# Gated attention and a feed-forward layer: K' turned by VectorE and DRAM instead of TensorE

## The chip, the cores and the metric

The kernel runs on one core of a Trainium2 chip. The metric is the device time of one launch in microseconds: 521.53 us in the median of three runs. The core has five engines that work side by side, each with a queue of its own in a fixed order: TensorE (PE, matrix products; its weight loads are shown as PEld), VectorE (DVE), ScalarE (ACT), GpSimd (POOL) and SyncE (SP), which here only issues transfers. Engines wait for each other by semaphores.

## The reference

```python
def _attn_ref(q, k, v, alpha):          # B, H, S, D = 4, 8, 768, 48
    for t in range(S):
        state = alpha[:, :, t, :, None] * state + np.einsum('bhd,bhe->bhde', k[:, :, t], v[:, :, t])
        y[:, :, t] = np.einsum('bhd,bhde->bhe', q[:, :, t], state)

def _moe_ref(x, w_in, w_out):           # 3072 x 384, 384 x 2048, 2048 x 384
    h = x @ w_in
    g = np.where(h >= 1, h, np.where(h <= -1, 0.0, (h + 1) ** 2 / 4))
    return g @ w_out
```

The output of the attention, laid as 3072 tokens of 384 numbers, is the x of the feed-forward layer. All inputs are fp32.

## The kernel before, in words

The 3072 tokens are 24 chunks of 128, counted from 0 here. For each chunk `prepare` loads alpha, k and q (`raw` tiles, eight buffers). From chunk 7 on (`EARLY`) they lie in DRAM with d at partitions; the chunks before are laid with the tokens at partitions, and `turned` transposes them on TensorE into PSUM (`flip`, L486). Two scans on VectorE make the running products of alpha, forward into `Q` (L547) and backward into `inv` (L573); `inv` times k is K' (L587) and `Q` times q is Q' (L593, POOL, or DVE in chunks 1 to 6).

The state update needs K' with tokens at partitions. `begin_chunk` transposes it on TensorE (`turn_keys`, L614, four matrix products against an identity), and ACT copies it from PSUM to the tile `ks` (L617). Then comes a burst of small products on TensorE: `update` (L642, `ks` with v), `scores` (L629) and, from chunk 7 on, the `outputs` (L769) of the chunk before. DVE adds the updates to `state` (L671) and masks the scores (L715); ACT and DVE split the outputs into two parts of fp32r in `ring` (L793, L798), and when a group of three chunks is complete six transfers within `ring` (L814) put the rest of it in its place.

The feed-forward layer works on groups of three chunks and sixteen blocks f of 128 hidden units. One step f is a hidden product on TensorE (`hidden`, L865: nine matrix products of 384 columns from `ring` into a `ps_h` bank), the activation (DVE clips, L909; ACT squares, L894; DVE takes the max, L920, into `gf`; ACT casts, L924, and POOL subtracts, L925, into `gh`), and a second product (`second`, L943: nine matrix products of `gh` with w_out). The second product of a step is given a due time `LAG` = 3 steps behind its hidden product, and `gf` and `gh` have three buffers. Groups 0 and 1 take eight blocks in turn, since the weights are still being fetched and decoded on ACT, DVE and POOL (L365 to L420); the others take sixteen.

What stands when on an engine is decided at build time: `Plan` collects all steps with a cost in us, a due time (in steps f) and what they read and write, and `order` runs a list scheduling over the five engines, with buffers, PSUM banks and the port that DVE and POOL share. Some steps may go to one of two engines (`other`). While TensorE would stand idle in the first part, fillers without use (L1014, `fill`) are put in its queue. SP issues all transfers in one queue.

Of the kernel before, what the change touches and what calls it, by code (L numbers as in the profile page):

```python
# [8 lines left out]
F32 = mybir.dt.float32  # L9
# [17 lines left out]
GROUP = 3  # L27
SHARE = 2
EARLY = 7
MORE = 2  # L30
WARM = 15
LAG = 3.0
FETCH = 12.0
LOAD = 4.0
DECODE = 3.0
PREPARE = 2.5
# [196 lines left out]
def gated_attention_ffn(ctx: ExitStack, tc: tile.TileContext, q, k, v, alpha, laid, out):  # L233
# [77 lines left out]
    with ExitStack() as main:  # L311
# [4 lines left out]
        def pool(name, **kw):  # L316
            pools[name] = main.enter_context(tc.tile_pool(name=name, bufs=1, **kw))
# [146 lines left out]
        def load(x, j, key):  # L464

            raw = raws[x, j] = buf("stage", "raw", [P, G * CH], 8)
            plan.op(
                "SP",
                Plan.ISSUE,
                key,  # L470
                lambda: nc.sync.dma_start(out=raw(), in_=laid[("tok_" if j < EARLY else "dim_") + x][j]),
                [],
                [raw],
                moved=P * G * CH * 4,
            )

        def turned(x, j, key, to=()):

            raw = raws[x, j]
            if j < EARLY:  # L480
                ps = ps_a(j)
                view = lambda: flat(ps())

                def flip():
                    for g in range(G):
                        nc.tensor.transpose(  # L486
                            out=view()[:, g * CH : (g + 1) * CH],
                            in_=raw()[:, g * P : (g + 1) * P],
                            identity=ident,
                        )  # L490
# [7 lines left out]
        def prepare(j, key):  # L498
# [85 lines left out]

            vec(0.15, lambda: nc.vector.reciprocal(out=meet[:, j, 1], in_=inv()[:, :, 0]), [inv], [("meet", j, 1)], False)
            kt, kT = turned("k", j, key + 0.2)
            vec(0.66, lambda: nc.vector.tensor_tensor(out=flat(inv()), in0=flat(inv()), in1=kT(), op=ALU.mult), [inv, kt], [inv])  # L587
# [5 lines left out]
            mul = lambda e: e.tensor_tensor(out=flat(Q()), in0=flat(Q()), in1=qT(), op=ALU.mult)  # L593
            in_ps = QHELP <= j < EARLY
            ways = [("DVE", 0.66, lambda: mul(nc.vector), not in_ps), ("POOL", 1.3, lambda: mul(nc.gpsimd), True)]
            (e, us, emit, port), other = ways if in_ps else reversed(ways)
# [4 lines left out]
        others, meets, turnt = {}, {}, {}  # L601
        group_of = [max(n for n in range(NG) if first[n] <= j) for j in range(NCH)]

        def begin_chunk(j, key):

            Q, K, _ = prepared[j]

            other = others[j] = buf("att", "other", [P, G, CH], 2)
            kp, ks = ps_a(j), buf("att", "ks", [P, G, P], 1)
            turnt[j] = ks  # L610

            def turn_keys():
                for g in range(G):
                    nc.tensor.transpose(out=kp()[:, g], in_=K()[:, g], identity=ident)  # L614

            plan.op("PE", 0.45, key - 0.1, turn_keys, [K], [kp, ks], mode="full")
            plan.op("ACT", 0.6, key, lambda: nc.scalar.copy(out=ks(), in_=kp()), [kp], [ks])  # L617

            meets[j] = [ps_a(j, 512) for _ in range(2)]
# [17 lines left out]
        def update(j):  # L637
            for g in range(G):
                for u in range(1 + ((j + 1) % PER != 0)):
                    for r in range(2):  # L640

                        nc.tensor.matmul(  # L642
                            out=up(j, u)[64 * r : 64 * r + 64, g],
                            lhsT=turnt[j]()[halves[u], g, 64 * r : 64 * r + 64],
                            rhs=V[j]()[halves[u], 2 * g + r],
                            start=True,
                            stop=True,
                        )
# [174 lines left out]
        def attend(j, key):  # L823

            begin_chunk(j, key)
            Q, K, _ = prepared[j]
            ks, vt = turnt[j], V[j]
            if j > MERGE:
                ps = ps_a(j)

# [21 lines left out]
        def hidden(n, f, key, c0=0, c1=GROUP):  # L852
# [1 line left out]
            c1 = min(c1, groups[n])  # L854
            L = (c1 - c0) * CH
            h = bank("ps_h", 2, [P, L])
            gf, gh = buf("fw", "gf", [P, L], 3), buf("fw", "gh", [P, 2, L], 3, F32R)
            xs = [("x", j % (2 * GROUP)) for j in range(first[n] + c0, first[n] + c1)]
            at = slice(span(n).start + c0, span(n).start + c1)

# [160 lines left out]
        for j in range(NCH):  # L1021
            n = max(n for n in range(NG) if first[n] <= j)
            since = begin[n - 1] if n > 0 else begin[n] - AHEAD
            due = since + (begin[n] - since) * (j - first[n] + 1) / groups[n] - (MARGIN, MARGIN0, MARGIN1)[n + 1 if n < 2 else 0]
            prepare(j, due - PREPARE)
            attend(j, due)
            done = j if j < MERGE or j == NCH - 1 else j - 1
            while at < len(segs) and first[segs[at][0]] + groups[segs[at][0]] - 1 <= done:
# [214 lines left out]
```

## Time and profile before

| | us |
|---|---|
| three runs: median (lowest to highest) | 521.53 (520.77 to 521.73) |
| span of the profiled execution, first to last instruction | 520.1 |
| PE busy in that span | 498.7 (96%) |
| DVE busy | 359.6 (69%) |
| ACT busy | 262.8 (51%) |
| POOL busy | 262.9 (51%) |

The profiled execution has no time of its own beside its span; the span is 1.4 us below the median of the runs. Busy times of PE are intervals that overlap, as its matrix products are pipelined, so what a piece of its work costs is read from starts: from one instruction's start to the next one's. In rows of a timeline the columns are start, length, engine, line, operation, output and inputs, count, and in brackets how long the engine stood idle before it and who ended that. In rows of groups they are count, busy us, mean ns, then idle time ahead. The granted clock of TensorE is 0.998 in the mean.

### The profile page before, as it was taken

The numbers are of one execution on the slowest core, as the hardware profiler recorded it, in microseconds if no ns is written. First come the engines' busy times: TensorE is split into PE (matmuls) and PEld (weight loads), VectorE is DVE, ScalarE is ACT, GpSimd is POOL, SyncE is SP. The second block draws the span as 40 slices with busy tenths as digits, with TensorE's granted clock in tenths as the row PEclk, the third lists the DMA queues.
The fourth block names the chain that finished last, engine by engine and source line by source line (L and its number), as shares of the span: only waits on it lengthen the run. The fifth ranks groups of instructions, "written<-read, shape, count | busy, mean of one in ns | idle before, by whom it ended". The sixth has DMA issues, their size and how long they took to land.

```text
span 520.1 us, 12248 instructions
## 1 busy us (share of the span) xinstructions
PE 498.7 (96%) x4861; PEld 480.4 (92%) x4861; DVE 359.6 (69%) x673; ACT 262.8 (51%) x509; POOL 262.9 (51%) x286
## 2 busy tenths in 40 slices
PE   8889898979999999999999999999999999999995
PEld 7788788978899999999999999999999999999994
DVE  6999999788978757578567757578567775343333
ACT  3899896575543444344444444444444444333331
POOL 3688885899974354254354344254354242323330
PEclk9999999999999999999999999999999999999999
DMA  8997849011435323133123323133102200010001
GB/s 255 378 348 250 316 98 346 3 48 55 122 106 137 109 65 90 48 96 122 43 60 91 112 62 79 56 84 125 56 21 59 67 2 11 15 37 10 0 1 50
DMA packets 27902, 52.46 MB, mean 101 GB/s; under 512 B 3808, under 2 KB 13504, under 8 KB 27840
## 3 DMA queue, kind: packets, MB, share of 16 engines
q1 hardware_dynamic: 27840, 51.62, 31.8%
q8 instruction: 40, 0.66, 0.6%
q14 instruction: 22, 0.18, 0.1%
HBM read 43.65 MB, written 5.90 MB: 95 GB/s over the span
## 4 chain that ended last, share of the span: by engine, by line
PE 79%; DVE 9%; POOL 4%; issue 3%; ACT 3%; DVEq 0%; POOLq 0%; ACTq 0%
PE ps L943 35%; PE ps L865 34%; PE ps L769 4%; PE ps L642 2%; DVE inv L573 2%; POOL gh L925 2%; PE ps L629 2%; PE ps L614 2%; DVE Q L547 1%; POOL w L405 1%; ACT gf L894 1%; DVE w L381 1%; DVE Q L715 1%; POOL wt L420 1%; PE ps L1014 1%
## 5 line engine op out<-in xcount | busy, mean ns | idle before, releaser
L943 PE MATMUL ps<-wt,gh 128*128 128x384 f32 x1152 | 225.3, 340 | 4.3 <-POOL gh L925 3.5
L925 POOL TENSOR_TENSOR gh<-gf,gh 128x384 fp32r<-128x384 f32 (+1 forms) x129 | 146.6, 1141 | 163.6 <-ACT gh L924 117.2
L865 PE MATMUL ps<-ring,wt 128*128 128x384 f32 (+1 forms) x1170 | 223.0, 337 | 2.8 <-DVE inv L573 1.2
L865 PEld LDWEIGHTS ps<-ring,wt 128*128 128x128 f32 x1170 | 203.9, 188 | 4.3 <-issue 1.5
L943 PEld LDWEIGHTS ps<-wt,gh 128*128 128x128 f32 x1152 | 200.5, 188 | 7.2 <-POOL gh L925 5.2
L894 ACT ACTIVATE gf<-gf,half_b 128x384 f32<-128x384 f32 x122 | 74.6, 616 | 120.7 <-DVE gf L909 117.4
L909 DVE TENSOR_SCALAR gf<-ps 128x384 f32<-128x384 f32 x122 | 66.9, 553 | 71.3 <-PE ps L865 62.7
L920 DVE TENSOR_TENSOR gf<-gf,ps 128x384 f32<-128x384 f32 (+1 forms) x130 | 70.3, 543 | 45.1 <-ACT gf L894 44.7
L924 ACT CAST gh<-gf 128x384 fp32r<-128x384 f32 (+1 forms) x130 | 65.7, 507 | 67.8 <-DVE gf L920 61.1
L573 DVE TENSOR_TENSOR_SCAN inv<-raw,bwd 128x511 f32<-128x511 f32 x17 | 34.9, 2052 | 0.0
L405 POOL TENSOR_TENSOR w<-w,wt 128x384 int32<-128x384 int32 (+1 forms) x25 | 31.2, 1261 | 7.0 <-DVE w L392 6.0
L547 DVE TENSOR_TENSOR_SCAN Q<-raw,fwd 128x512 f32<-128x512 f32 x17 | 27.4, 1613 | 7.3 <-PE ps L769 7.2
L420 POOL TENSOR_TENSOR wt<-w,wt 128x384 fp32r<-128x384 f32 (+1 forms) x24 | 31.3, 1318 | 1.7 <-ACT wt L418 1.4
L661 ACT COPY both<-state 48x192 f32<-48x192 f32 x69 | 24.1, 350 | 12.3 <-POOL state L746 9.0
L746 POOL TENSOR_TENSOR state<-state,last 128x192 f32<-128x192 f32 x20 | 11.9, 594 | 34.3 <-DVE state L671 34.1
L769 PE MATMUL ps<-Q,both 128*64 128x64 f32 x372 | 27.1, 225 | 1.4 <-issue 1.4
L769 PEld LDWEIGHTS ps<-Q,both 128*64 128x64 f32 x372 | 23.7, 137 | 4.1 <-issue 2.8
L769 PE MATMUL ps<-other,both 128*64 128x64 f32 x372 | 27.0, 225 | 0.0
L617 ACT COPY ks<-ps 128x512 f32<-128x512 f32 x24 | 14.1, 587 | 21.5 <-PE ps L614 21.4
L715 DVE TENSOR_TENSOR Q<-ps,mask 64x256 f32<-64x256 f32 x48 | 20.3, 423 | 6.5 <-ACT other L679 5.6
L593 POOL TENSOR_TENSOR Q<-Q,raw 128x512 f32<-128x512 f32 x18 | 23.2, 1290 | 2.9 <-DVE inv L565 2.0
L769 PEld LDWEIGHTS ps<-other,both 128*64 128x64 f32 x372 | 23.5, 138 | 0.2 <-ACT both L661 0.2
(79 smaller groups left out, 415.7 us busy)
## 6 DMA issues: line engine op xcount, KB each, us to landing
both<-in_laid_v_both SPq DMA_DIRECT2D x48, 128.0 KB, 3.0
wt<-in_laid_w_in SPq DMA_DIRECT2D x8, 768.0 KB, 7.2
wt<-in_laid_w_out SPq DMA_DIRECT2D x8, 768.0 KB, 7.5
vt<-in_laid_v SPq DMA_DIRECT2D x24, 192.0 KB, 2.9
out<-ot SPq DMA_DIRECT2D x24, 192.0 KB, 2.7
raw<-in_laid_dim_a SPq DMA_DIRECT2D x17, 256.0 KB, 2.9
raw<-in_laid_dim_k SPq DMA_DIRECT2D x17, 256.0 KB, 3.0
raw<-in_laid_dim_q SPq DMA_DIRECT2D x17, 256.0 KB, 2.7
```

The costliest lines, as they stand in the source:

```text
L405: add = lambda e, c=c: e.tensor_tensor(out=bits()[:, c], in0=bits()[:, c], in1=word(I32, 0)[:, c], op=ALU.add)
L420: sub = lambda e, c=c: e.tensor_tensor(out=part(1)[:, c], in0=data()[:, c], in1=part(0).bitcast(F32)[:, c], op=ALU.subtract)
L547: lambda: nc.vector.tensor_tensor_scan(flat(Q()), aT(), flat(fwd), 0.0, ALU.mult, ALU.max),
L573: lambda: nc.vector.tensor_tensor_scan(flat(inv())[:, 0:n][:, ::-1], aT()[:, 1 : n + 1][:, ::-1], flat(bwd)[:, 0:n][:, ::-1], bwd[:, G - 1 ...
L769: nc.tensor.matmul(out=ps()[halves[r], to, halves[u]], lhsT=lhsT[:, r, u], rhs=x()[:, g, halves[u]], start=m + u == 0, stop=True, skip_gro ...
L865: nc.tensor.matmul(out=h(), lhsT=win(f, w)[:, kt], rhs=ring[:, at, kt, a, :], start=(m == 0), stop=(m == 3 * KT - 1),)
L894: lambda: nc.scalar.activation(out=gf(), in_=in_(), func=func, scale=scale, bias=bias),
L909: lambda: nc.vector.tensor_scalar(out=gf(), in0=h(), scalar1=-1.0, scalar2=1.0, op0=ALU.max, op1=ALU.min),
L920: lambda: nc.vector.tensor_tensor(out=gf(), in0=gf(), in1=h(), op=ALU.max),
L924: plan.op("ACT", 0.08 + 0.41 * w, key + 0.4, lambda: nc.scalar.copy(out=gh()[:, 0], in_=gf()), [gf], [gh])
L925: sub = lambda e: e.tensor_tensor(out=gh()[:, 1], in0=gf(), in1=gh()[:, 0].bitcast(F32), op=ALU.subtract)
L943: nc.tensor.matmul(out=o_ps[seg][t](), lhsT=gh()[:, a, (t - c0) * CH : (t - c0 + 1) * CH], rhs=wout(f, w), start=(f == f0 and i == 0), sto ...
```

## The change

K' of chunks 7 to 23 (`TURN` = 7) is no longer turned by TensorE and ACT. `turn_blocks` transposes its sixteen 32x32 blocks on DVE into a tile `part` (L622 of the changed file), writes `part` to a buffer in DRAM (256 KB, L634) and reads it back with four transfers of 32 partitions each, in runs of 512 bytes, into `ks` (L644), which now has two buffers and another order of its columns. All five are issued by SP. The chunks from 7 on are prepared 2.5 steps earlier (`PLACING`). k and q of chunks 2 to 6 are laid with d at partitions, so that only alpha of these chunks is flipped on TensorE; their Q' may now go to DVE or POOL. `LAG` is 4, and `gf` and `gh` have four buffers. The scratch memory that the program reserves for transfers is made smaller.

```diff
+PLACED = {"a": EARLY, "k": 2, "q": 2}
+TURN = 7
+PLACING = 2.5
-LAG = 3.0
+LAG = 4.0
...
+        blocks = [pools["sums"].tile([P, G * CH], F32, name=f"blocks{i}") for i in range(2)]
...
-                lambda: nc.sync.dma_start(out=raw(), in_=laid[("tok_" if j < EARLY else "dim_") + x][j]),
+                lambda: nc.sync.dma_start(out=raw(), in_=laid[("tok_" if j < PLACED[x] else "dim_") + x][j]),
...
-            if j < EARLY:
+            if j < PLACED[x]:
...
-            in_ps = QHELP <= j < EARLY
+            in_ps = QHELP <= j < PLACED["q"]
...
+        def turn_blocks(j, K, ks, key):
+            part = buf("att", "part", [P, 4, 32, G], 1)
+            plan.op(
+                "DVE",
+                0.62,
+                key - PLACING,
+                lambda: nc.vector.transpose(
+                    out=part().rearrange("p j b g -> p j g b"), in_=K().rearrange("p g (j a) -> p j g a", a=32)
+                ),
+                [K],
+                [part],
+                port=True,
+            )
+            placed = lambda: ks().rearrange("p g c -> p (g c)").rearrange("p (c g) -> p c g", g=G)
...
+                lambda: nc.sync.dma_start(out=blocks[j % 2], in_=part().rearrange("p j b g -> p (j b g)")),
...
+            for i in range(4):
...
+                    lambda i=i: nc.sync.dma_start(
+                        out=ks()[32 * i : 32 * i + 32],
+                        in_=blocks[j % 2].rearrange("(i a) (j c) -> j a i c", a=32, c=CH)[i],
+                    ),
...
+            turnt[j] = lambda u, g, r: placed()[halves[u], 64 * r : 64 * r + 64, g], ks
...
-            kp, ks = ps_a(j), buf("att", "ks", [P, G, P], 1)
+            ks = buf("att", "ks", [P, G, P], 2)
+            if j >= TURN:
+                return turn_blocks(j, K, ks, key)
...
-            gf, gh = buf("fw", "gf", [P, L], 3), buf("fw", "gh", [P, 2, L], 3, F32R)
+            gf, gh = buf("fw", "gf", [P, L], 4), buf("fw", "gh", [P, 2, L], 4, F32R)
...
-            prepare(j, due - PREPARE)
+            prepare(j, due - PREPARE - PLACING * (j >= TURN))
...
-    nc = bacc.Bacc("TRN2", target_bir_lowering=False, num_devices=1)
+    nc = bacc.Bacc("TRN2", target_bir_lowering=False, num_devices=1, dynamic_dma_scratch_size=1024)
```

With it the planner's order changes on all engines. First PE around the burst of chunk 14, before (L943 second products, L865 hidden ones, L614 the turn, L642 and L629 the start of the burst):

```order
L943 MATMUL ps<-wt,gh 128x384 x9
L865 MATMUL ps<-ring,wt 128x384 x18
L943 MATMUL ps<-wt,gh 128x384 x18
L865 MATMUL ps<-ring,wt 128x384 x9
L614 MATMUL ps<-ident,inv 128x128 x4
L943 MATMUL ps<-wt,gh 128x384 x9
L865 MATMUL ps<-ring,wt 128x384 x9
L642 MATMUL ps<-vt,ks 64x48 x16
L629 MATMUL ps<-Q,inv 64x64 x16
```

and the same place in the changed kernel (L996 second, L918 hidden, L694 and L681 the start of the burst):

```order
L996 MATMUL ps<-wt,gh 128x384 x9
L918 MATMUL ps<-ring,wt 128x384 x9
L996 MATMUL ps<-wt,gh 128x384 x18
L918 MATMUL ps<-ring,wt 128x384 x18
L996 MATMUL ps<-wt,gh 128x384 x9
L918 MATMUL ps<-ring,wt 128x384 x9
L996 MATMUL ps<-wt,gh 128x384 x9
L694 MATMUL ps<-vt,ks 64x48 x16
L681 MATMUL ps<-Q,inv 64x64 x16
```

The turn is gone, and the burst stands behind the 59th hidden product instead of the 58th.

Then DVE between two bursts, where the first row belongs to the burst's state update and L587 makes K', before (a cycle with the forward scan L547 right behind that update; L715 are the masks):

```order
L671 TENSOR_TENSOR state<-state,ps 128x192
L909 TENSOR_SCALAR gf<-ps 128x384
L551 RECIPROCAL bwd<-Q 128x4
L565 COPY inv<-bwd 128x1
L573 SCALAR_TENSOR_TENSOR inv<-raw,bwd 128x511
L920 TENSOR_TENSOR gf<-gf,ps 128x384
L909 TENSOR_SCALAR gf<-ps 128x384
L585 RECIPROCAL meet<-inv 128x4
L920 TENSOR_TENSOR gf<-gf,ps 128x384
L587 TENSOR_TENSOR inv<-inv,raw 128x512
```

and after, where L962 is the clip, L973 the max, L577 the backward scan, L593 K' and L622 the transposition:

```order
L723 TENSOR_TENSOR state<-state,ps 128x192
L555 RECIPROCAL bwd<-Q 128x4
L569 COPY inv<-bwd 128x1
L962 TENSOR_SCALAR gf<-ps 128x384 x2
L577 SCALAR_TENSOR_TENSOR inv<-raw,bwd 128x511
L589 RECIPROCAL meet<-inv 128x4
L593 TENSOR_TENSOR inv<-inv,raw 128x512
L973 TENSOR_TENSOR gf<-gf,ps 128x384 x2
L622 STREAM_TRANSPOSE part<-inv 128x4x4x32
```

Two clips stand ahead of the backward scan instead of one, none behind it, and the maxes behind K' instead of ahead. In other cycles with ten products one max stands between K' and the transposition.

SP's queue over the same cycle, before:

```order
L519 DMA both<-in_laid_v_both 64x512 x2
L508 DMA vt<-in_laid_v 128x384
L471 DMA raw<-in_laid_dim_q 128x512
L471 DMA raw<-in_laid_dim_a 128x512
L471 DMA raw<-in_laid_dim_k 128x512
L519 DMA both<-in_laid_v_both 64x512 x2
L508 DMA vt<-in_laid_v 128x384
```

and after:

```order
L523 DMA both<-in_laid_v_both 64x512 x2
L512 DMA vt<-in_laid_v 128x384
L475 DMA raw<-in_laid_dim_q 128x512
L475 DMA raw<-in_laid_dim_a 128x512
L475 DMA raw<-in_laid_dim_k 128x512
L634 DMA blocks_108<-part 128x512
L644 DMA ks<-blocks_108 32x4x128 x4
L523 DMA both<-in_laid_v_both 64x512 x2
```

The write and the four reads stand behind the three loads of the next chunk and ahead of the loads of v that wait for the burst.

Last, PE at the start of the group of chunks 9 to 11, behind the burst of chunk 12 (its last product is the first row), before:

```order
L769 MATMUL ps<-other,both 64x64
L865 MATMUL ps<-ring,wt 128x384 x9
L943 MATMUL ps<-wt,gh 128x384 x9
L865 MATMUL ps<-ring,wt 128x384 x9
L943 MATMUL ps<-wt,gh 128x384 x9
L865 MATMUL ps<-ring,wt 128x384 x18
```

and after:

```order
L821 MATMUL ps<-other,both 64x64
L918 MATMUL ps<-ring,wt 128x384 x9
L996 MATMUL ps<-wt,gh 128x384 x27
L918 MATMUL ps<-ring,wt 128x384 x27
L996 MATMUL ps<-wt,gh 128x384 x9
```

The first product of the new group is the second half of the last row before and the first third of the row of 27 after: five products stood between burst and group, now four.

More of the change, by code (lines that the diff above doesn't have):

```diff
@@ L586, in prepare @@
             kt, kT = turned("k", j, key + 0.2)
-            vec(0.66, lambda: nc.vector.tensor_tensor(out=flat(inv()), in0=flat(inv()), in1=kT(), op=ALU.mult), [inv, kt], [inv])
+            vec(
+                0.66,
+                lambda: nc.vector.tensor_tensor(out=flat(inv()), in0=flat(inv()), in1=kT(), op=ALU.mult),
+                [inv, kt],
+                [inv],
+                j >= PLACED["k"],
+            )
             qt, qT = turned("q", j, key + 0.2)
@@ L593, in prepare @@
             mul = lambda e: e.tensor_tensor(out=flat(Q()), in0=flat(Q()), in1=qT(), op=ALU.mult)
-            in_ps = QHELP <= j < EARLY
+            in_ps = QHELP <= j < PLACED["q"]
             ways = [("DVE", 0.66, lambda: mul(nc.vector), not in_ps), ("POOL", 1.3, lambda: mul(nc.gpsimd), True)]
-            (e, us, emit, port), other = ways if in_ps else reversed(ways)
+            (e, us, emit, port), other = ways if QHELP <= j < EARLY else reversed(ways)
             plan.op(e, us, key + 0.3, emit, [Q, qt, last], [Q], port=port, other=None if in_ps else other)
@@ L602, in gated_attention_ffn @@
         group_of = [max(n for n in range(NG) if first[n] <= j) for j in range(NCH)]
+        def turn_blocks(j, K, ks, key):
[10 more added lines that the diff above has]
+                port=True,
+            )
+            placed = lambda: ks().rearrange("p g c -> p (g c)").rearrange("p (c g) -> p c g", g=G)
+            plan.op(
+                "SP",
+                Plan.ISSUE,
+                key - PLACING,
+                lambda: nc.sync.dma_start(out=blocks[j % 2], in_=part().rearrange("p j b g -> p (j b g)")),
+                [part],
+                [("blocks", j % 2)],
+                moved=P * G * CH * 4,
+            )
+            for i in range(4):
+                plan.op(
+                    "SP",
+                    Plan.ISSUE,
+                    key - PLACING,
+                    lambda i=i: nc.sync.dma_start(
+                        out=ks()[32 * i : 32 * i + 32],
+                        in_=blocks[j % 2].rearrange("(i a) (j c) -> j a i c", a=32, c=CH)[i],
+                    ),
+                    [("blocks", j % 2)],
+                    [ks],
+                    moved=P * CH * 4,
+                    beside=i > 0,
+                )
+            turnt[j] = lambda u, g, r: placed()[halves[u], 64 * r : 64 * r + 64, g], ks
         def begin_chunk(j, key):
@@ L608, in begin_chunk @@
             other = others[j] = buf("att", "other", [P, G, CH], 2)
-            kp, ks = ps_a(j), buf("att", "ks", [P, G, P], 1)
-            turnt[j] = ks
+            ks = buf("att", "ks", [P, G, P], 2)
+            if j >= TURN:
+                return turn_blocks(j, K, ks, key)
+            kp = ps_a(j)
+            turnt[j] = lambda u, g, r: ks()[halves[u], g, 64 * r : 64 * r + 64], ks
             def turn_keys():
@@ L617, in begin_chunk @@
             plan.op("ACT", 0.6, key, lambda: nc.scalar.copy(out=ks(), in_=kp()), [kp], [ks])
-            meets[j] = [ps_a(j, 512) for _ in range(2)]
         ss = lambda j, r: meets[j][r]()[:, 0 : G * HC].rearrange("p (g t) -> p g t", g=G)
@@ L643, in update @@
                             out=up(j, u)[64 * r : 64 * r + 64, g],
-                            lhsT=turnt[j]()[halves[u], g, 64 * r : 64 * r + 64],
+                            lhsT=turnt[j][0](u, g, r),
                             rhs=V[j]()[halves[u], 2 * g + r],
@@ L825, in attend @@
             begin_chunk(j, key)
+            meets[j] = [ps_a(j, 512) for _ in range(2)]
             Q, K, _ = prepared[j]
-            ks, vt = turnt[j], V[j]
+            ks, vt = turnt[j][1], V[j]
             if j > MERGE:
```

## The prediction

> **What bounds the kernel now.** I read four stretches first, then who TensorE waits for. The columns are length, busy time of PE, its weight loads, DVE, ACT and POOL, clock, DMA share and GB/s.
>
> ```profile
> 0.00:80.00 80.00, 71.55 (x1029) 63.92 (x1030) 71.86 (x135) 65.05 (x127) 56.96 (x80) 1.00 0.82 277
> 80.00:140.00 60.00, 53.06 (x462) 49.91 (x461) 52.14 (x80) 37.75 (x67) 52.80 (x38) 1.00 0.31 105
> 140.00:440.00 300.00, 300.00 (x2952) 293.19 (x2951) 206.74 (x406) 133.60 (x268) 130.82 (x147) 1.00 0.26 75
> 440.00:520.00 80.00, 74.06 (x424) 73.33 (x422) 28.86 (x54) 26.39 (x47) 22.34 (x22) 0.99 0.07 20
> ```
>
> From 140 us TensorE is busy throughout, at full clock; whatever it no longer does there comes off the end. Before 140 us no engine is full: DVE, ACT and POOL hand work round and TensorE waits, between 80 and 135 us at these seven places.
>
> ```profile
> 84.89 0.61 PE L943 MATMUL ps<-wt,gh 128*128 128x384 f32 x2 [0.74 <-ACT gh L924]
> 86.17 3.06 PE L943 MATMUL ps<-wt,gh 128*128 128x384 f32 x16 [0.67 <-POOL gh L925]
> 101.45 0.68 PE L642 MATMUL ps<-vt,ks 64*64 64x48 f32 x32 [0.75 <-ACT ks L617]
> 112.96 1.49 PE L943 MATMUL ps<-wt,gh 128*128 128x384 f32 x7 [2.42 <-POOL gh L925]
> 116.80 1.50 PE L943 MATMUL ps<-wt,gh 128*128 128x384 f32 x7 [0.43 <-POOL gh L925]
> 129.06 3.05 PE L865 MATMUL ps<-ring,wt 128*128 128x384 f32 x16 [0.65 <-POOL wt L420]
> 133.32 0.66 PE L614 MATMUL ps<-ident,inv 128*128 128x128 f32 x4 [1.22 <-DVE inv L587]
> ```
>
> Together 6.9 us. One chunk's cycle in the full stretch, from the chain that ended last (start, length, what):
>
> ```profile
> 253.18 0.61 PE ps L642 x32
> 253.79 0.48 PE ps L629 x32
> 255.35 1.77 PE ps L943 x9
> 257.12 1.57 PE ps L865 x9
> ...
> 269.71 1.57 PE ps L865 x9
> 271.28 0.44 PE ps L614 x4
> 271.72 1.60 PE ps L943 x9
> 273.32 0.61 PE ps L642 x32
> ```
>
> A burst takes 2.17 us (253.18 to 255.35), the first product behind it 1.77, each other 1.57. The turn of K' (L614) takes 0.44 and makes the product behind it 0.03 longer: 0.47 us. Without it a cycle of 10 products is 2.17 + 1.77 + 9 x 1.57 = 18.07 us, of 11 19.64, of 12 21.21.
>
> **The change, part by part.** *Turns of K'.* 17 of 24 go, all behind 90 us: 17 x 0.47 = -8.0. Their evictions on ACT (L617) lay beside products and are worth nothing.
>
> *What takes their place* is a chain: transposition on DVE, a write to DRAM, four reads queued behind it on SP, then the burst. Its start is tied to the burst before, since the forward scan L547 writes the Q buffer which that burst reads last. DVE and POOL in such a cycle, whose burst began at 291.29:
>
> ```profile
> 291.29 0.68 PE L642 MATMUL ps<-vt,ks 64*64 64x48 f32 x32
> 293.56 1.62 DVE L547 TENSOR_TENSOR_SCAN Q<-raw,fwd 128x512 f32<-128x512 f32 x1 [0.72 <-PE ps L769]
> 297.58 0.35 DVE L671 TENSOR_TENSOR state<-state,ps 128x192 f32<-128x192 f32 x1
> 298.60 2.67 DVE L573 TENSOR_TENSOR_SCAN inv<-raw,bwd 128x511 f32<-128x511 f32 x1
> 298.89 1.29 POOL L593 TENSOR_TENSOR Q<-Q,raw 128x512 f32<-128x512 f32 x1
> 303.39 0.69 DVE L587 TENSOR_TENSOR inv<-inv,raw 128x512 f32<-128x512 f32 x1
> 303.99 1.01 DVE L909 TENSOR_SCALAR gf<-ps 128x384 f32<-128x384 f32 x2
> ...
> L573 DVE TENSOR_TENSOR_SCAN inv<-raw,bwd 128x511 f32<-128x511 f32 x17 | 34.9, 2052 | 0.0
> L381 DVE TENSOR_SCALAR w<-w 128x768 int32<-128x768 int32 x16 | 13.9, 869 | 0.4 <-ACT w L365 0.4
> ```
>
> The backward scan began 7.3 us behind the burst. The new order has one more clip ahead of it (half of 1.01): 7.8. With its mean of 2.05 it ends at 9.85; L585 and K's product (0.17 and 0.69) bring 10.7, one max 0.5 more, 11.2. No transposition stands in the trace: it lies between 512/768 of L381's 0.87, 0.58 us, and the scan's 2.05. I take 0.65, near the copy-like row, as it has one input. It ends at 11.9.
>
> The trip has no row either. The nearest transfers (count, KB, median us from issue to landing; out is written to DRAM), the spread of out's landings, and two rows of SP's issues:
>
> ```profile
> out<-ot SPq DMA_DIRECT2D x15, 192.0 KB, 2.6
> raw<-in_laid_dim_k SPq DMA_DIRECT2D x11, 256.0 KB, 2.8
> both<-in_laid_v_both SPq DMA_DIRECT2D x26, 128.0 KB, 2.7
> ring<-ring SPq DMA_DIRECT2D x30, 48.0 KB, 2.2
> ...
> DMA to landing us min/median/max: 1.9/2.7/3.9
> ...
> 304.10 0.33 SPq L471 DMA_DIRECT2D raw<-in_laid_dim_k  x1
> 219.09 3.87 SPq L814 DMA_DIRECT2D ring<-ring  x6
> ```
>
> The write is 256 KB: 2.8. The reads are 64 KB each, issued back to back as ring's six (3.87 / 6 = 0.65 apart): the fourth starts 1.95 later and lands after some 2.4, between ring and both. 7.2 us in all; at least 1.9 + 3 x 0.33 + 2.2 = 5.1, at most 3.9 + 1.95 + 3.9 = 9.8. So K' is there 11.9 + 7.2 = 19.1 us behind the burst before, and a burst after 10 products waits 1.0. By the new order, of the 15 cycles between the bursts of chunks 8 and 23 (counted from 0), seven have 10 products, six have 11 and two have 12. Seven times 1.0 is 7.0; with 11 products one more max stands ahead (19.6 against 19.64), I take 0.2 each, 1.2; with 12 the transposition stands two or three steps later, I take 0.7 each, 1.4. Sum +9.6. At the short trip it is 0, at the long one over 35; the middle rows were picked because sizes and back-to-back issue match them. Behind a late K' stands the whole burst, and with it all of PE's queue; SP's reads wait on the write, but the loads behind them are needed only a cycle later.
>
> The write to DRAM landed no later than the loads: out 2.6, raw 2.8. [...]
>
> *Group starts.* In the two groups that begin behind the bursts of chunks 9 and 12 four products stand between burst and first hidden product, before five. The same place before:
>
> ```profile
> 214.41 0.68 PE L642 MATMUL ps<-vt,ks 64*64 64x48 f32 x32
> 223.00 3.30 PE L865 MATMUL ps<-ring,wt 128*128 128x384 f32 x18
> ```
>
> The six transfers of ring began at 219.09 (above); the last starts 5 x 0.65 later and lands after 2.2, at 224.5, 10.1 behind the burst. The first product that reads it began at 223.00 + 1.57 = 224.57: no slack. One product fewer leaves 2.17 + 1.77 + 3 x 1.57 = 8.65: 1.45 late, twice: +2.9 (0 if those DMAs go out earlier than I think).
>
> *Lag 4 and four g buffers* give each second product one more step (3.14 us) of cover. Of the 6.9 us of waits above, four of the seven are for gh, 4.3 us. POOL is busy 52.8 of 60 there, so part is lack of throughput, which depth does not mend; three transpositions come on top of DVE's 52.1. I take -2, from -6.9 (all waits go) to nothing.
>
> *Chunks 2 to 6.* 40 flips leave PE, but 51 more idle fillers stand in its order:
>
> ```profile
> L486 PE MATMUL ps<-ident,raw 128*128 128x128 f32 x84 | 12.8, 292 | 0.7 <-PE ps L943 0.4 <-DMA raw<-in_laid_tok_a 0.2
> L1014 PE MATMUL ps<-zeros 128*128 128x256 bf16 x69 | 10.5, 305 | 1.1 <-DVE zeros L247 1.1
> L593 DVE TENSOR_TENSOR Q<-Q,ps 128x512 f32<-128x512 f32 x6 | 4.1, 678 | 0.0
> ```
>
> -40 x 12.8/84 + 51 x 10.5/69 = +1.7 of PE, in a stretch where PE waits anyway. Four products of Q move from DVE (-4 x 0.68 = -2.7) to POOL (+4 x 1.29 = +5.2). Between -2.7 and +5.2; I take 0, the two engines being about as loaded there (71.9 and 57.0 of 80).
>
> *Sum:* -8.0 + 9.6 + 2.9 - 2 + 0 = +2.5 on the span of 520.1, 522.6; the runs' median lies 1.4 above that span: **524.0**.
>
> **Rivals.** *The trip fits, and it is faster.* If the trip takes under 6.2 us (18.07 - 11.9), no burst waits: 521.5 - 8.0 - 2 + 2.9 = 514.4. For it: a lone issue costs 0.33, and out has landed in 1.9. Against: four issues in a row have never been 0.33 apart. It breaks even near 7.0, where the waits sum to 7.1 (7 x 0.8 + 6 x 0.1 + 2 x 0.45). *A late early stretch:* POOL's extra 5.2 us push decoding and gh, so that the stretch before 140 us loses 3 instead of gaining 2: 529.0. For it speaks that POOL is the releaser in four of the seven waits. *A slow write:* at the longest landing, 3.9, each trip is 1.1 longer: 7 x 2.1 + 6 x 1.1 + 2 x 1.8 = 24.9 instead of 9.6, giving 539.3. Against: 2.6 is out's median.
>
> That the turns stay is no rival: in the order L668 stands 28 times, not 96.
>
> **How the numbers follow.** Forecast 0.42, its own range 520.5 to 528 (ten-product waits of 0.7 to 1.3); the trip fits, or nearly, 0.36; early stretch 0.14; slow write 0.08. The range takes in the fitting trip with a little of the early gain, 513, and the early loss with the forecast's upper end, 533. About 0.2% (1.0 us) is what a measurement of this kernel tells from no change: of the forecast 0.10 lies within it. Faster 0.36, same 0.10, slower 0.32 + 0.14 + 0.08 = 0.54.
>
> **What would show it.** Right: a row in which L694 waits for DMA ks<-blocks, near 1 us, some seven to fifteen times; two waits of L918 for DMA ring near 1.4; the wait for POOL gh (L978) below 4; cycles of 18.1 us plus the wait. Wrong: no such rows, PE without gaps from 140 us; then the trip is shorter than 6.2. The landing rows of blocks and ks, and the transposition's row, size each term.

## The result and the profile after

The changed kernel takes 526.02 us in the median of twelve runs (523.74 to 528.91); the kernel before took 521.50 us in twelve runs beside it. The ratio is 1.008 [1.0064, 1.0096]: slower by 0.8%. The profiled execution is the fastest of the twelve: 523.74 us, a span of 522.0, 1.9 more than before. The granted clock of the twelve is 0.984 to 1.000, 0.9955 in the median; it is 1.000 in the profiled one.

The four stretches of the changed kernel, as they were shown of the kernel before:

```profile
0.00:80.00 80.00, 71.50 (x1018) 61.14 (x1019) 72.67 (x136) 63.05 (x122) 62.16 (x85) 1.00 0.84 279
80.00:140.00 60.00, 54.09 (x404) 51.46 (x406) 50.83 (x77) 36.53 (x64) 55.40 (x41) 1.00 0.35 118
140.00:440.00 300.00, 299.83 (x2924) 293.43 (x2921) 212.04 (x422) 130.70 (x265) 121.65 (x136) 1.00 0.34 101
440.00:520.00 80.00, 77.76 (x469) 76.70 (x468) 29.85 (x56) 26.97 (x48) 22.31 (x22) 1.00 0.07 20
```

The busy time of TensorE between 80 and 140 us is no lower than before (54.09 against 53.06), but the work there is done later. Behind 48 products of nine matrix products in both kernels, the burst of chunk 8 begins here before:

```profile
137.05 0.68 PE L642 MATMUL ps<-vt,ks 64*64 64x48 f32 x32
```

and here in the changed kernel, 2.1 us later:

```profile
139.13 1.05 PE L694 MATMUL ps<-vt,ks 64*64 64x48 f32 x28
```

From 140 us on TensorE is still busy throughout. Whom does it wait for there? The whole answer of the waits, 140 to 520 us (us in total, times, longest):

```profile
PE ps L918 <- DMA ring<-ring: 0.2, 1, 0.2
```

That one wait is at the start of a group, the one behind the burst of chunk 9 (160.84). Six matrix products go ahead, the others of that product wait:

```profile
169.88 1.22 PE L918 MATMUL ps<-ring,wt 128*128 128x384 f32 x6
171.28 2.33 PE L918 MATMUL ps<-ring,wt 128*128 128x384 f32 x12 [0.17 <-DMA ring<-ring]
```

No burst waits for K'. One cycle, from the timeline (start, length, engine, line, operation); the first row is the burst before:

```profile
277.88 1.17 PE L694 MATMUL ps<-vt,ks 64*64 64x48 f32 x32
285.17 1.29 POOL L603 TENSOR_TENSOR Q<-Q,raw 128x512 f32<-128x512 f32 x1
286.11 1.43 DVE L577 TENSOR_TENSOR_SCAN inv<-raw,bwd 128x511 f32<-128x511 f32 x1
288.86 1.12 DVE L622 STREAM_TRANSPOSE part<-inv 128x512 f32<-128x512 f32 x1
290.00 0.33 SPq L634 DMA_DIRECT2D blocks<-part  x1
293.04 1.75 SPq L644 DMA_DIRECT2D ks<-blocks  x4
296.45 1.27 PE L694 MATMUL ps<-vt,ks 64*64 64x48 f32 x32
```

The transposition ends at 289.98, 12.1 behind the burst before (forecast 11.9). The write goes out at once, the reads at 293.04, each 1.75 / 4 = 0.44 behind the last; the fourth starts at 294.4 and lands some 2.0 later, at 296.4: a trip of 6.4 us, not 7.2. This is the longest trip of the seven cycles with ten products, in which K' has least time; the other six took 5.3 to 6.2 us. Over all 15 trips from 140 us on it was 5.3 to 7.2, 5.8 in the median. The median landings, 160 to 420 us:

```profile
blocks<-part SPq DMA_DIRECT2D x13, 256.0 KB, 2.2
ks<-blocks SPq DMA_DIRECT2D x52, 64.0 KB, 2.0
```

Yet the cycle is 18.57 us (277.88 to 296.45), half a microsecond over the 18.07 of a cycle without any wait. The chain of work that ended last shows where, since there each piece lasts until the next begins:

```profile
296.52 1.16 PE ps L694 x31
297.68 0.52 PE ps L681 x25
298.20 1.08 PE ps L821 x32
```

The first piece of the burst, the update, takes 1.16 us here and 1.10 in most bursts; before it was L642 with 0.61. The groups of that line in the kernel before, with weight loads (PEld) and products (count, busy us, mean ns):

```profile
L642 PE MATMUL ps<-vt,ks 64*64 64x48 f32 x704 | 16.1, 221 | 0.7 <-ACT ks L617 0.7
L642 PEld LDWEIGHTS ps<-vt,ks 64*64 64x64 f32 x704 | 13.4, 134 | 5.3 <-issue 3.9 <-ACT ks L617 1.1 <-ACT other L679 0.3
```

The same two groups of the changed kernel:

```profile
L694 PE MATMUL ps<-vt,ks 64*64 64x48 f32 x704 | 24.9, 265 | 0.3 <-ACT ks L671 0.2
L694 PEld LDWEIGHTS ps<-vt,ks 64*64 64x64 f32 x704 | 22.1, 188 | 5.3 <-issue 4.1 <-ACT ks L671 0.7 <-ACT other L731 0.2
```

The same count of instructions of the same shape, but the load of 64x64 weights from `ks` costs 54 ns more in the mean over all chunks. The new `ks` holds the four g of one column side by side, so the 64 columns that one load reads lie four elements, 16 bytes, apart. Between 140 and 440 us, where nearly every `ks` is of that kind, the median load is 213 ns, against 135. Over a group of three chunks and 32 products the cycle is 58.83 us before (253.11 to 311.94) and 58.98 after (296.45 to 355.43): the turn's 0.47 us is gone three times, and 0.52 has come in its place three times.

In the two profiled executions this adds up as follows. The burst of chunk 8 stands 2.1 us later than before, that of chunk 23 4.8 us (429.66 and 434.44), with one product of 1.57 us more done ahead of it. At equal work the stretch between the two is so 1.1 longer: 15 times 0.05, the wait of 0.2, and 0.2 more. What lies behind chunk 23 is 1.3 shorter at equal work; why was not looked into. Together that is the 1.9 of the spans. The other 2.6 us of the 4.5 between the medians stand in no trace, since the profiled execution is the fastest of the twelve.

### The profile page after: what moved, and what is told of

It reads as the page before. It is cut to its first block, busy times and chain, and to the rows that moved or that the text cites. A ratio compares the mean times of both kernels' runs of the same rounds, so it can differ in the third digit from the quotient of the medians.

```text
span 522.0 us, 12253 instructions
## 1 busy us (share of the span) xinstructions
PE 503.2 (96%) x4804; PEld 482.7 (92%) x4804; DVE 365.4 (70%) x688; ACT 257.2 (49%) x498; POOL 261.5 (50%) x282
## 4 chain that ended last, share of the span: by engine, by line
PE 73%; DVE 8%; POOL 8%; DMA 5%; issue 3%; SPq 1%; ACT 1%; POOLq 0%; DVEq 0%; ACTq 0%
PE ps L918 33%; PE ps L996 32%; PE ps L821 4%; PE ps L694 3%; DMA raw<-in_laid_dim_k 3%; POOL wt L424 2%; POOL gh L978 2%; POOL w L409 2%; PE ps L681 2%; DVE w L396 1%; DMA wt<-in_laid_w_in 1%; DMA raw<-in_laid_tok_a 1%; DVE w L385 1%; DVE Q L767 1%; DVE Q L551 1%
## 5 line engine op out<-in xcount | busy, mean ns | idle before, releaser
L918 PE MATMUL ps<-ring,wt 128*128 128x384 f32 (+1 forms) x1170 | 222.6, 337 | 4.0 <-DVE ot L344 1.6
L996 PE MATMUL ps<-wt,gh 128*128 128x384 f32 x1152 | 221.6, 338 | 4.0 <-POOL gh L978 2.4
L978 POOL TENSOR_TENSOR gh<-gf,gh 128x384 fp32r<-128x384 f32 (+1 forms) x127 | 134.3, 1061 | 176.9 <-ACT gh L977 157.4
L918 PEld LDWEIGHTS ps<-ring,wt 128*128 128x128 f32 x1170 | 203.1, 188 | 6.9 <-DVE ot L344 2.0
L996 PEld LDWEIGHTS ps<-wt,gh 128*128 128x128 f32 x1152 | 201.3, 188 | 7.0 <-POOL gh L978 3.4
L962 DVE TENSOR_SCALAR gf<-ps 128x384 f32<-128x384 f32 x122 | 67.5, 554 | 59.5 <-PE ps L918 58.9
L973 DVE TENSOR_TENSOR gf<-gf,ps 128x384 f32<-128x384 f32 (+1 forms) x130 | 70.3, 544 | 50.2 <-ACT gf L947 49.7
L713 ACT COPY both<-state 48x192 f32<-48x192 f32 x76 | 26.7, 351 | 41.4 <-POOL state L798 39.1
L424 POOL TENSOR_TENSOR wt<-w,wt 128x384 fp32r<-128x384 f32 (+1 forms) x26 | 36.4, 1408 | 1.8 <-DVE fwd L541 0.9
L409 POOL TENSOR_TENSOR w<-w,wt 128x384 int32<-128x384 int32 (+1 forms) x24 | 32.3, 1358 | 5.8 <-DVE w L396 4.8
L603 POOL TENSOR_TENSOR Q<-Q,raw 128x512 f32<-128x512 f32 x22 | 28.7, 1305 | 3.9 <-DVE inv L569 2.4
L551 DVE TENSOR_TENSOR_SCAN Q<-raw,fwd 128x512 f32<-128x512 f32 x17 | 22.2, 1307 | 8.1 <-PE ps L821 8.1
L694 PEld LDWEIGHTS ps<-vt,ks 64*64 64x64 f32 x704 | 22.1, 188 | 5.3 <-issue 4.1
L577 DVE TENSOR_TENSOR_SCAN inv<-raw,bwd 128x511 f32<-128x511 f32 x17 | 25.2, 1483 | 0.0
L694 PE MATMUL ps<-vt,ks 64*64 64x48 f32 x704 | 24.9, 265 | 0.3 <-ACT ks L671 0.2
```

The costliest lines, as they stand in the source:

```text
L409: add = lambda e, c=c: e.tensor_tensor(out=bits()[:, c], in0=bits()[:, c], in1=word(I32, 0)[:, c], op=ALU.add)
L424: sub = lambda e, c=c: e.tensor_tensor(out=part(1)[:, c], in0=data()[:, c], in1=part(0).bitcast(F32)[:, c], op=ALU.subtract)
L694: nc.tensor.matmul(out=up(j, u)[64 * r : 64 * r + 64, g], lhsT=turnt[j][0](u, g, r), rhs=V[j]()[halves[u], 2 * g + r], start=True, stop=True,)
L918: nc.tensor.matmul(out=h(), lhsT=win(f, w)[:, kt], rhs=ring[:, at, kt, a, :], start=(m == 0), stop=(m == 3 * KT - 1),)
L962: lambda: nc.vector.tensor_scalar(out=gf(), in0=h(), scalar1=-1.0, scalar2=1.0, op0=ALU.max, op1=ALU.min),
L973: lambda: nc.vector.tensor_tensor(out=gf(), in0=gf(), in1=h(), op=ALU.max),
```

## The experiments

All times are medians; each ratio is against the kernel before, run beside it on the same chip, with a 95% interval. Theory A: the stride costs what the turns gave. Theory B, the prediction's: K' itself comes late. Theory C: neither, the loss is elsewhere.

**1. The stride taken away, nothing else moved.**

```diff
-            turnt[j] = lambda u, g, r: placed()[halves[u], 64 * r : 64 * r + 64, g], ks
+            turnt[j] = lambda u, g, r: ks()[halves[u], g, 64 * r : 64 * r + 64], ks
```

> The changed kernel with one thing different: the update (L694) reads K' as if its columns lay one behind another, not four elements apart, so it multiplies the right numbers in the wrong order; every instruction, transfer and wait stays. Theory A (the stride of the weights costs 0.5 us a burst, and K' is there in time): the 32 rows of L694 take 0.6 us again instead of 1.1, cycles of 10 products fall from 18.57 to 18.07 us, and the time falls by 17 x 0.5 = 8.5 us, to about 517.5 against 526 for the changed kernel, so 0.992 of the kernel before. Theory B (K' itself comes only 18.5 us behind the burst before, and the slow weight load hides that): cycles of 10 products stay near 18.5 and show a wait of L694 for ks or a gap before it, 11-product cycles fall to 19.64; the fall is only 8 to 10 times 0.5, about 521.5, a ratio near 1.0. Theory C (the stride is harmless, the loss is elsewhere): no change, ratio 1.008.

517.44 us, ratio 0.9917 [0.9894, 0.9940], 8.6 us below the changed kernel (6.6 between the two profiled executions). The update is as short as before, in its group:

```profile
L694 PE MATMUL ps<-vt,ks 64*64 64x48 f32 x704 | 16.4, 222 | 0.3 <-ACT ks L671 0.2
```

Its timeline at a burst that begins 18.09 us behind the one before (274.37):

```profile
285.99 0.33 SPq L634 DMA_DIRECT2D blocks<-part  x1
288.95 1.75 SPq L644 DMA_DIRECT2D ks<-blocks  x4
292.46 0.68 PE L694 MATMUL ps<-vt,ks 64*64 64x48 f32 x32
```

Theory A, and B falls: from 140 us on no row has L694 wait for `ks`; the only wait of TensorE is one of 0.5 us for ring. K' starts its trip half a microsecond earlier too, since the scan that leads to it waits for the burst before, and its last read lands (288.95 + 3 x 0.44 + 2.0 = 292.3) just ahead of the burst. In the seven cycles with ten products it lands 0.1 to 1.2 us ahead. A group of 32 products takes 57.41 us (292.46 to 349.87), 1.42 less than before: 0.47 for each turn, as the prediction had it.

**2. The stride alone.** The kernel before, in which ACT writes `ks` with that stride.

```diff
-            plan.op("ACT", 0.6, key, lambda: nc.scalar.copy(out=ks(), in_=kp()), [kp], [ks])
+            plan.op("ACT", 0.6, key, lambda: nc.scalar.copy(out=placed(), in_=kp()), [kp], [ks])
...
-                            lhsT=turnt[j]()[halves[u], g, 64 * r : 64 * r + 64],
+                            lhsT=turnt[j][1]()[halves[u], g, 64 * r : 64 * r + 64],
```

> The kernel before, with TensorE still turning K', but ScalarE's eviction writes it four elements apart as the changed kernel has it, and the update reads it so in all 24 chunks. Theory A: each burst gets 0.5 us longer, 18 of them in the full stretch, some also before it: +9 to +12 us, ratio 1.017 to 1.023. Theory C: the same time, ratio 1.000, apart from an eviction on ScalarE that may take longer than 0.6 us beside other work.

534.36 us, ratio 1.0235 [1.0214, 1.0255]: +12.6 for 24 chunks, 0.52 each; one stretch at half clock (see below) is in it, but a group of 32 products, free of such, takes 60.46 us (281.84 to 342.30), 1.63 or 3 x 0.54 more than before. The weight loads of the line (ns: least, median, most):

```profile
L643 PEld LDWEIGHTS ps<-vt,ks x704: 188/213/215, 11.9 to 443.4; 64*64 64x64 f32 x176
```

ACT's copy, a group of the same kernel; the kernel before needs 587 ns for it:

```profile
L618 ACT COPY ks<-ps 128x512 f32<-128x512 f32 x24 | 26.3, 1095 | 23.3 <-PE ps L615 23.2
```

The stride is a price by itself, and it is paid by the writer too. No burst waits for that longer copy from 140 us on.

**3 to 6. The parts, one by one.** Runs 3, 4 and 6 are the changed kernel but for what is named here; 5 is the kernel before with two numbers changed. All four, 5 too, have the smaller scratch memory.

```diff
 e3: +TURN = 99                                  # all K' turned by TensorE
 e4: +LAG = 3.0, three g buffers, PLACED = EARLY # only the blocks
 e5: +LAG = 4.0, four g buffers                  # only these
 e6: +TURN = 99, LAG = 3.0, three g buffers      # only q and k laid with d at partitions
```

> All of the change but the blocks: q and k of chunks 2 to 6 laid with d at partitions, products one step more apart, four g buffers; K' of all chunks turned by TensorE. My forecast gave this part -2 us (519.5, ratio 0.996). From the sum after the fact (-8.0 for the turns, +8.5 for the stride, +1.9 in the profiled span, more in the median) it should cost 1.4 to 4: ratio 1.003 to 1.008, with the loss before 140 us or in a lower granted clock.

> Only the blocks: K' of chunks 7 to 23 by VectorE and DRAM; q and k of chunks 2 to 6 turned on TensorE as before, the distance of the products and three g buffers as before. Theory A: -8.0 for the turns, +8.5 for the stride, and waits of 0.2 to 0.7 at group starts: ratio 1.001 to 1.004, cycles of 10 products 18.57. Theory B as in the first run: the same number, by waits for ks. If the blocks carry all of the loss, 1.008.

> The kernel before with products one step more apart and four g buffers, nothing else of the change. My forecast gave this -2 us (ratio 0.996, from 0.987 to 1.000). Theory D (the 6.6 us that the early parts cost together come from the four products of Q that move to POOL, which delay the decoding of weights): this part is harmless, ratio 0.996 to 1.000. Theory E (the later second products leave TensorE without work while the weights are still decoded, at chunks 7 and 8): ratio 1.006 to 1.013, and fewer products done by 150 us than the 54.9 of the kernel before.

> The kernel before with k and q of chunks 2 to 6 laid with d at partitions, nothing else of the change. My forecast gave this 0 us, from -2.7 to +5.2. Theory D: it carries the loss, +4 to +6.6 us, ratio 1.008 to 1.013, with waits for POOL wt that the kernel before has not. Theory E: ratio 0.998 to 1.003.

| | us | ratio | burst of chunk 8, at 48 products | half-clock stretches before 200 us |
|---|---|---|---|---|
| before | 521.5 | | 137.0 | none |
| changed kernel | 526.0 | 1.0080 [1.0064, 1.0096] | 139.1 | none in the profiled run |
| 4: blocks only | 536.55 | 1.0284 [1.0262, 1.0306] | 141.0 | 3.4 us |
| 5: distance 4, four g buffers | 526.53 | 1.0077 [1.0051, 1.0104] | 140.7 | 3.4 + 6.8 us |
| 6: q and k laid anew | 525.66 | 1.0063 [1.0043, 1.0082] | 140.9 | 6.8 + 3.4 us |
| 3: both of 5 and 6 | 528.42 | 1.0123 [1.0102, 1.0143] | 145.8 | 3.4 + 3.4 + 6.8 us |

The fourth column counts products of nine matrix products that stand ahead of that burst: all six kernels have done the same 48, so these times compare. Theory D had the whole loss of the early parts with run 6, theory E with run 5: each holds some of it. The smaller scratch memory is not the cause: run 10 below has it, and its early part is that of before. Run 4 is far above what was expected of it (1.001 to 1.008), and run 3 above its range. Every part alone makes the kernel slower, and the parts do not add: by the medians, each against the kernel before beside it, 4.8 + 3.9 + 14.8 = 23.5, together 4.5. The order is planned anew each time. With the old distance the blocks pay the stride and waits as well. The waits of run 4 on PE from 170 us on:

```profile
PE ps L694 <- DMA ks<-blocks: 2.5, 3, 1.7
```

and those of its weight loads from 140 us on:

```profile
PEld ps L996 <- POOL gh L978: 3.0, 8, 0.5
PEld ps L694 <- DVE gf L973: 2.0, 1, 2.0
```

The late K' of the prediction is there. The longest of its waits, 1.7, stands behind a write to DRAM that landed only after 5.1 us (the median of that run is 2.0). There are also 76 fillers (L1067) between 123 and 155 us, 8.8 us of TensorE. These waits are 7.5 of the 14.8 us at most; the rest was not taken apart. That it is the distance of 4 that lets the blocks fit in the changed kernel is likely, but no run separates it from the new laying of q and k; alone it costs.

**What follows an idle place in the early part.** The windows of run 5 around its second half-clock stretch (busy time of PE, PEld, DVE, ACT, POOL, then the granted clock):

```profile
127.77:131.18 3.41, 3.41 (x21) 3.41 (x21) 3.38 (x4) 1.59 (x3) 3.24 (x4) 1.00 0.05 17
131.18:134.59 3.41, 0.94 (x6) 0.61 (x4) 2.73 (x3) 0.74 (x2) 3.02 (x2) 1.00 0.77 250
134.59:141.42 6.83, 4.26 (x37) 3.42 (x38) 4.03 (x9) 4.51 (x10) 6.16 (x4) 0.50 0.00 0
141.42:144.83 3.41, 3.41 (x89) 3.27 (x86) 1.90 (x3) 1.84 (x4) 1.26 (x3) 1.00 0.12 23
```

Where TensorE was busy for 0.94 of 3.41 us, the next 6.83 us run at half clock (0.50 in their row). In the traces of the twelve experiments there are 20 such stretches ahead of the last products, 3.41 or 6.83 us long; in the 3.41 us before 19 of them TensorE was busy for 13 to 50% (before one, 64%). The reverse holds nearly as well: counted in steps of 3.41 us from a stretch (the two of run 7 begin at 57.69 and 122.54 us, 19 steps of 3.413 apart), one window as idle had no such stretch behind it (run 5 from 49.26 us, 1.61 us busy). Run 5 has 10.2 us at half clock. In run 7 seven matrix products of 384 columns took 2.61 us at half clock (from 122.90) and 1.49 at full clock (from 119.75); so the 10.2 us cost an estimated half of that at most, 5.1, and less where TensorE waits anyway; run 9 below bounds it.

**7. The right order without a stride.** The transposition writes `part` plainly, four writes and four reads in runs of 128 bytes bring K' to its place.

```diff
-            part = buf("att", "part", [P, 4, 32, G], 1)
+            part = buf("att", "part", [P, 4, G, 32], 1)
...
-                    out=part().rearrange("p j b g -> p j g b"), in_=K().rearrange("p g (j a) -> p j g a", a=32)
+                    out=part(), in_=K().rearrange("p g (j a) -> p j g a", a=32)
...
+                for i in range(4):
+                    nc.sync.dma_start(
+                        out=runs[i].rearrange("j a c -> a j c"),
+                        in_=part()[32 * i : 32 * i + 32].rearrange("a j g b -> a j (g b)"),
+                    )
...
+                        out=ks()[:, :, 32 * i : 32 * i + 32],
+                        in_=runs[i].rearrange("j a (g b) -> (j a) g b", b=32),
```

> The changed kernel with K' placed one column behind another in the right order: the block transposition writes its output without a stride, four writes of 64 KB put it in DRAM, and the four reads bring runs of 128 bytes. The order on PE, DVE, ACT and POOL is that of the changed kernel; SP issues three transfers more per chunk. Theory A with room in the trip: L694 takes 0.6 us, time as in the first run of this study, about 517.5, ratio 0.992. If the trip has no room (its reads were done just about at the burst): three issues of 0.44 us and shorter runs make K' 1.5 to 3 us late in cycles of 10 products, waits of L694 for ks appear, and the time is 520 to 530.

522.08 us, ratio 0.9995 [0.9974, 1.0017]: in the range of the second expectation, though by another way than many late K'. The weights load in 135 ns, cycles of 10 products are 18.1, and the transposition, whose output had the stride too, is shorter. Its group in the changed kernel:

```profile
L622 DVE STREAM_TRANSPOSE part<-inv 128x512 f32<-128x512 f32 x17 | 18.8, 1105 | 0.2
```

and in this one:

```profile
L622 DVE STREAM_TRANSPOSE part<-inv 128x512 f32<-128x512 f32 x17 | 11.9, 702 | 0.2
```

K' is now late twice, 1.2 us in all from 140 us on, and the early part lost again: 48 products at 140.8, two half-clock stretches in it (57.7 and 122.5 us), where run 1, in the same order on PE, has none and is there at 138.8.

**8. Without the fillers.**

```diff
-        plan = Plan(lambda n: fill(n))
+        plan = Plan(lambda n: None)
```

> The changed kernel with the 105 idle fillers taken out that the planner had put in the first 70 us (the 15 at the start stay); the order of all else is the same. If fillers cost time (TensorE's work was ready earlier than planned): 1 to 4 us less than the changed kernel, ratio 1.000 to 1.006. If they only fill waits: the same 526, ratio 1.008. If the granted clock needs them: a clock below 1.0 in the first 100 us and a longer time, ratio 1.010 to 1.02.

528.28 us, ratio 1.0127 [1.0105, 1.0150], 2.3 above the changed kernel: the 105 fillers cost nothing on balance. Without them the clock falls in the first 35 us (0.86 from 0 to 20 us, 0.80 from 20 to 40), where the changed kernel has 1.00. Around the first of three half-clock stretches:

```profile
10.90:14.31 3.41, 1.55 (x60) 1.19 (x52) 3.22 (x9) 1.91 (x5) 0.99 (x3) 1.00 0.98 375
14.31:21.14 6.83, 6.09 (x118) 5.55 (x119) 3.91 (x7) 4.20 (x9) 3.48 (x6) 0.50 0.96 337
```

This is the only change made for the clock. In the profiled run of the changed kernel two windows of 3.41 us, from 54.68 and from 119.5 us, had TensorE busy for 1.76 us each, 52%, and no half clock followed. Whether other runs of that kernel have half clock behind these two places, and scatter for it (523.7 to 528.9), no trace shows; over the twelve runs clock and time go together only loosely (527.84 us at 0.996).

**9. The distance without the later decoding.** The number for the distance also sets when w_out is due to be decoded.

```diff
-                decode(u, "o", to, wo[u], ready + LAG)
+                decode(u, "o", to, wo[u], ready + 3.0)
```

> The kernel before with products one step more apart and four g buffers, as in the run of that part alone (526.5 us), but w_out decoded as early as the kernel before has it: in that run the due time of its decoding (line 460 of the changed kernel, ready + LAG) moved one step later too. Theory G (the waits of L943 for wt, 7.0 us there against none in the kernel before, come from that later decoding): the waits for wt go, and with them the half-clock stretches behind them; 520 to 522.5, ratio 0.996 to 1.002. Theory E (the order of the products itself costs it): 526, ratio 1.006 to 1.010.

522.86 us, ratio 1.0023 [1.0014, 1.0033], 3.7 less than run 5. Between 80 and 140 us run 5 had these waits for decoded weights, and this run has none for wt:

```profile
PE ps L943 <- ACT wt L418: 3.1, 1, 3.1
PE ps L943 <- POOL wt L420: 2.9, 2, 1.9
```

Close to theory G's time (0.4 over its end), though one wait of 3.1 us for K' (L614 for inv) has come instead. The half-clock stretches did not go, as theory G had it: run 9 has 10.2 us at half clock too, and yet is only 1.4 above before. So it is not the clock that explains run 5; most of its loss came with the later decoding.

**10. The early part as before, blocks from chunk 9 on.** K' goes as in run 7; the lines are against that run.

```diff
+TURN = 9
+LAG = (3.0, 4.0)    # from the third group on 4, and four g buffers
+PLACED = {"a": EARLY, "k": EARLY, "q": EARLY}
```

> The first 100 us as in the kernel before (its planner's numbers, q and k of chunks 2 to 6 turned on TensorE, three g buffers and a distance of 3 for the first two groups), blocks with contiguous K' from chunk 9 on, distance 4 and four g buffers from the third group on. If the turns are worth 0.47 each once the stride is gone, and the early stretch stays as it was: -15 x 0.47 = -7.0 and some 0.5 for the trip, about 515, ratio 0.987 (0.984 to 0.992). If the early loss comes back (the planner puts 8 fillers more, and K' of chunks 9 and 10 crowds DVE): 518 to 522, ratio 0.993 to 1.000.

522.35 us, ratio 1.0023 [1.0009, 1.0038], above both expectations. The early part is that of before to 0.1 us (48 products at 137.1, no half-clock stretch). It is lost where the first blocks come, 135 to 180 us:

```profile
PE ps L920 <- DMA ring<-ring: 1.5, 1, 1.5
PE ps L695 <- DMA ks<-blocks: 1.2, 1, 1.2
PE ps L998 <- POOL wt L425: 0.9, 1, 0.9
```

Three of the six transfers of ring went out 1.5 us behind the others, since SP issued three loads of partial sums (L1028) between them; the product waits for these. That is the 1.5 us that the prediction gave a group's start, but by another way than the one product fewer that it counted. After 180 us K' is late twice more, 1.5 us in all.

**11. A stride of 8 bytes.** The lines are against run 7.

```diff
-            part = buf("att", "part", [P, 4, G, 32], 1)
+            part = buf("att", "part", [P, 4, 2, 32, 2], 1)
...
+            placed = lambda: ks().rearrange("p g c -> p (g c)").rearrange("p (h d l) -> p h d l", h=2, l=2)
+            turnt[j] = lambda u, g, r: placed()[halves[u], g // 2, 64 * r : 64 * r + 64, g % 2], ks
```

> As the run with contiguous K' (522.1 us), but with K' two elements (8 bytes) apart instead of one: transposition output and weights with a stride of 8 bytes, reads in runs of 256 bytes. If any stride costs, or the cost grows with it: weight loads of L694 between 135 and 213 ns, 32 rows of L694 in 0.75 to 0.9 us, the transposition between 0.70 and 1.1 us, the time 1.5 to 4 us above the contiguous run, ratio 1.003 to 1.008. If only the stride of 16 bytes costs: 135 ns, 0.70 us, ratio 0.998 to 1.001. [...]

520.90 us, ratio 0.9996 [0.9979, 1.0013], the second expectation; K' is late four times, 1.3 us in all. The weight loads:

```profile
L695 PEld LDWEIGHTS ps<-vt,ks x704: 129/135/140, 11.3 to 432.0; 64*64 64x64 f32 x176
```

and the transposition:

```profile
L622 DVE STREAM_TRANSPOSE part<-inv x17: 656/706/715, 86.0 to 423.5; 128x512 f32<-128x512 f32 x17
```

8 bytes cost nothing; 16 bytes cost 78 ns more on a load of 135, and 0.40 us more on a transposition of 0.70. So the step lies between 8 and 16 bytes, for fp32 weights and for what DVE writes; for what ACT writes only the 16 bytes were run.

**12. A version put together.** The lines are against run 11; the four g buffers stay.

```diff
+PLACING = 4.0
+LAG = 3.0
+PLACED = {"a": EARLY, "k": 7, "q": 7}
-            plan.op("SP", Plan.ISSUE, key - PLACING, write, ...
+            plan.op("SP", 2.0, key - PLACING, write, ...
```

> A version put together from the runs: blocks from chunk 7 on with K' 8 bytes apart (as in the run with that stride), chunks prepared 4 steps earlier instead of 2.5, products at the distance of 3 as in the kernel before, four g buffers, q and k of chunks 2 to 6 turned on TensorE as before, and the planner told that the four writes take 2 us of SP. If the turns' 0.47 us come through and K' is in time, as in the run in which the update read K' in another order: -8.0 and some early loss, 514 to 518, ratio 0.987 to 0.993. If K' is late behind the closer products (waits of L695 for ks near 0.5 to 1 us in many bursts, as in the run of the blocks alone): 520 to 525, ratio 0.997 to 1.007.

527.44 us, ratio 1.0112 [1.0082, 1.0143]: the second expectation, and worse than its end. With the old distance bursts wait again, from 140 us on:

```profile
PE ps L695 <- DMA ks<-blocks: 3.6, 5, 1.3
PE ps L695 <- DVE gf L974: 2.0, 1, 2.0
PE ps L997 <- POOL gh L979: 1.2, 3, 0.5
```

No version but run 1, whose update takes K's columns in another order, beat the kernel before. Run 1 shows what this order of work would gain if K' came in place without three more transfers per chunk: 517.4, about 4 us.

## Why the prediction was right and wrong

The sign was right, and 526.0 lies in its range, 2.0 above the number. That was luck: the term that made it slower, 9.6 us of waits for K', did not come at all, and a cost of 8.6 us that the sum did not have stood in its place. By the prediction's own sign of being wrong (no such rows, TensorE without gaps from 140 us) the rival of the fitting trip had the mechanism right, and that rival gave 514.4.

- *Turns, -8.0:* right. Without the stride a chunk is 0.47 us shorter (run 1).
- *Bursts wait for K', +9.6:* wrong in the changed kernel, 0.0. Its transposition took 1.1 us instead of 0.65, but the backward scan 1.48 in the mean (L577) instead of 2.05, so the chain ended at 12.1 as against 11.9 in the cycle shown (why the scan was shorter was not tried). The trip was the mis-sized term: the write landed in 2.2 in the median, not 2.8, the reads went out 0.44 apart, not 0.65, and landed in 2.0, not 2.4; 5.8 us in the median and 6.4 in the cycle shown, instead of 7.2. The rival had put the point from which no burst waits at 6.2. In run 1, where the cycle is half a microsecond shorter, the chain ended at 11.6 and the trip of the cycle shown took 6.3, so even that one fits, with 0.2 to spare. The slow write does not show in the median, 2.2; single writes did land late, after up to 3.7 us here and 5.1 in run 4.
- *What the sum lacked:* the new order of K's columns. The text names runs of 512 bytes and another order of the columns, and priced neither what writes with that stride nor what reads with it. It is +0.5 for each of 17 chunks, 8.6 us by the medians (runs 1 and 2), nearly the 9.6 that stood there for another reason.
- *Group starts, +2.9:* 0.2 from 140 us on and one of 0.6 ahead of it, in the changed kernel. The sum took it that the new group's first product waits as a whole for the last of the six transfers; six of its nine matrix products, 1.2 us, went ahead of the wait. The longer burst hid part of the rest: run 1, without the stride, waits once 0.5.
- *Distance and buffers, -2:* wrong by its sign. Alone +4.8 (run 5). The step took the distance for cover only; the same number made w_out's decoding late (run 9: 3.7 us of the 4.8). In the changed kernel the burst of chunk 8 stands 2.1 us later than before, with 48 products done in both.
- *Chunks 2 to 6, 0 (from -2.7 to +5.2):* +3.9 alone (run 6), within the ends given. The rival of the late early stretch, 529.0, named a loss of 3 ahead of 140 us: it was 2.1 in the profiled run of the changed kernel; the other runs have no trace.
- The pieces were added as if each kept its size. Measured alone they sum to 23.5 us, together they are 4.5.

The profiled execution also flattered the change: its span was 1.9 us above that of before, while the medians are 4.5 apart. Where the other 2.6 are lost stays open.

## What to carry to other kernels

When data takes a new way to a tile, price the instructions that read and write its new layout, element by element in bytes, before pricing the way: 16 bytes between columns cost as much here as the whole saving. In a kernel that a list scheduler orders, a number such as a distance may set other due times as well, so look up all its uses, and do not add the effects of parts that were planned apart. Compare two orders by when the same count of products is done, not by busy shares, which hid the 2.1 us lost before 140 us here.

## What the runs showed of the hardware

- fp32 elements 16 bytes apart: weight loads of 64x64 213 ns instead of 135, a 128x512 block transposition on DVE 1105 instead of 702, a 128x512 copy on ACT 1095 instead of 587. Elements 8 bytes apart: 135 for the weights and 705 for the transposition.
- The granted clock is 1.0 or 0.5 here; ahead of the last products the stretches at 0.5 are 3.41 or 6.83 us long, and 19 of 20 stand behind 3.41 us in which TensorE was busy for half or less. Those 3.41 us need not be idle: half clock followed 1.55 us of work in run 8.
- 256 KB written to DRAM and read back in four parts that were issued behind it took 5.3 to 7.2 us, 5.8 in the median of 15 trips of the changed kernel.
- The backward scan on DVE (128x511) took 1.27 us with no POOL work beside it (changed kernel, from 385.31 us), and 2.07 and 2.94 us with POOL busy throughout (kernel before, from 282.31 and 128.99). The planner reckons with a port that the two share; the traces show the longer times, and no run tried their reason.
